# Pooling attention followed by mixture-of-depths: value pooling placed ahead of a gather, exponentials written contiguously, the second layer in one job, another order for batch 0

## The chip, the cores and the metric

The kernel runs on one core of a Trainium2 chip. Its engines are TensorE (PE: matmul; PEld: weight load), VectorE (DVE), ScalarE (ACT), GpSimd (POOL) and SyncE (SP); each works through its own instructions in order. The metric is the device time of one execution in microseconds (us); the median of the runs is compared.

## The reference

All values are fp32. B = 8 batches, H = 8 heads, S = 576 positions, D = 64, F = 1024, capacity 128.

```python
k_p = k.reshape(B, H, Sp, 8, D).mean(axis=3)         # 576 keys -> 72
v_p = v.reshape(B, H, Sp, 8, D).mean(axis=3)
attn = softmax(q @ k_p.T / sqrt(D)) @ v_p            # (B, H, S, D)
x = attn.transpose(0, 2, 1, 3).reshape(B, S, 512)
scores = x @ w_gate                                  # (B, S)
out = x.copy()
for b in range(B):
    top = the 128 positions with the largest scores[b]
    ye = relu(x[b, top] @ w1) @ w2                   # 512 -> 1024 -> 512
    out[b, top] = x[b, top] + sigmoid(scores[b, top])[:, None] * ye
```

## The kernel before, in words

The order of all instructions is written by hand; nothing is rescheduled. Batches go in pairs, an even one e and an odd one o. Each pair takes five steps u: two steps of 256 positions for e, one that holds the last 64 positions of both batches, and two steps of 256 positions for o. In step u the main loop runs the attention of that step (`attend`, L352, on PE into an accumulator pA, of which there are two; `norm`, L360 to L377, on DVE), then the jobs of slot 0, then the scores of step u+1 (`scores`, L323: PE writes four PSUM banks, ACT takes exponentials of them, eight instructions at L338), the stores of x, the transposes of q for step u+2 (L308), and the jobs of slots 1 to 4. A job is put in a slot of a step by `at(u, slot, job, ...)`; jobs of a slot run in the order in which they were put.

Per batch the jobs are these. `pool_k` (L230, L231, POOL) and `k_trans` (L236 to L242, DVE) make pooled keys. `pool_v` (L248 to L252, POOL) adds eight values of each of four heads; half 0 and half 1 are the two groups of four heads. Its last instruction (L252) multiplies by w_gate, and `gate_v` (L256, DVE) sums that product into the column of the tile vp that `attend` reads with the pooled values. When a batch's scores for the gate are complete, `row_bcast` (L416, PE) and `count` (L428 to L433, DVE) rank its 576 positions, holding an accumulator pA; `one_hot` (L440, PE; L441, L443, DVE) and `gather` (L451, PE; L453, DVE, tile tok; L455, POOL, tile idx; L457, an indirect DMA issued by POOL) fetch the 128 chosen rows from the output in DRAM into xr. `gate` (L467, DVE) and `x_trans` (L479, PE; copied to xg by ACT at L481) follow; then the dense jobs: `hidden` twice (L489, PE; relu at L491, ACT) and `finish` twice, 256 columns each (L502, PE; y at L503, DVE), and the scatter of y (L505, an indirect DMA on POOL's queue). Loads of k, q and v are issued by SP (v: L122, L123), stores of x by ACT.

Of the kernel before, what the change touches and what calls it, by code (L numbers as in the profile page):

```python
# [10 lines left out]
AF = mybir.ActivationFunctionType  # L11
OP = mybir.AluOpType
# [36 lines left out]
def direct_path(ctx, tc, q, k, v, moe_w_gate, moe_w1, moe_w2, moe_capacity, out, flag):  # L49
# [27 lines left out]
    G = 16  # L77
# [163 lines left out]
        nc.vector.tensor_reduce(out=y[:, :, 0:128:2], in_=x[:, :, 0:64, :], axis=AX.X, op=OP.add)  # L241
        nc.vector.tensor_reduce(out=y[:, :, 1:128:16], in_=x[:, :, 64:SP, :], axis=AX.X, op=OP.add)  # L242

    def pool_v(b, g, eng):
        x = VR[b, g]
        VP[b] = vps[b % 2]
        h = slice(HG * g, HG * g + HG)
        eng.tensor_tensor(out=x[:, :, 0:4, :], in0=x[:, :, 0:4, :], in1=x[:, :, 4:8, :], op=OP.add)  # L248
        eng.tensor_tensor(out=x[:, :, 0:2, :], in0=x[:, :, 0:2, :], in1=x[:, :, 2:4, :], op=OP.add)  # L249
        eng.tensor_tensor(out=VP[b][:, h, 0:D], in0=x[:, :, 0, :], in1=x[:, :, 1, :], op=OP.add)  # L250

        nc.gpsimd.tensor_tensor(out=x[:, :, 2, :], in0=VP[b][:, h, 0:D], in1=wg[:, h, :], op=OP.mult)  # L252
# [58 lines left out]
    def scores(u):  # L311
        b = steps_all[u][0]
        if b is None:
            parts = [(x, slice(QT4 * n, QT4 * n + QT4)) for n, x in enumerate(lasts(u))]
        else:
            parts = [(b, slice(0, TM))]
        p = [bank([128, 2, len(parts), G * (parts[0][1].stop)], i) for i in range(4)]
        for n, (x, t) in enumerate(parts):
            for s in range(2):
                for j in range(2):  # L320
                    for i in range(4):
                        r = slice(32 * i, 32 * i + 32)
                        nc.tensor.matmul(p[i][:, s, n, :], KT[x][r, j, s, :], QT[u][r, j, t, G * s : G * s + G],  # L323
                                         start=(j == 0), stop=(j == 1))
        if b is None:
            ET[u] = [work.tile([128, 2, len(parts), TL], FT, name=f"el{i}{len(parts)}") for i in range(4)]
            for i in range(4):
                nc.scalar.activation(ET[u][i].rearrange("p s n (g t) -> p (s n) g t", t=QT4),
                                     p[i].rearrange("p s n (t g) -> p (s n) g t", t=QT4), AF.Exp, scale=exp_scale)
        else:  # L330
            ET[u] = [[work.tile([128, 2, C], FT, name=f"et{i}{c}") for i in range(4)] for c in range(2)]
            for c in range(2):
                for i in range(4):
                    x = p[i].rearrange("p s one (n t c g) -> p (s one n) c g t", n=2, c=2, g=G)[:, :, c]
                    y = ET[u][c][i].rearrange("p s (n g t) -> p (s n) g t", n=2, g=G)
                    if c == 0:
                        x, y = (z.rearrange("p a g t -> p a t g") for z in (x, y))
                    nc.scalar.activation(y, x, AF.Exp, scale=exp_scale)  # L338

    def attend(a):  # L340
        u, x = chunks[a]
# [92 lines left out]

    def one_hot(b):

        p = accumulator()[:, 0, 0 : 2 * NC].rearrange("p (k c) -> p k c", k=2)
        for c in range(NC):
            for i in range(c, NC):
                nc.tensor.matmul(p[:, 0, c : c + 1], GE[b][i][:, c, :], ones, start=(i == c), stop=(i == NC - 1))  # L440
        nc.vector.tensor_tensor(out=p[:, 1, :], in0=CN[b], in1=p[:, 0, :], op=OP.subtract)  # L441
        OH[b] = work.tile([C, NC, cap], BF, name="oh", bufs=1)
        nc.vector.tensor_tensor(  # L443
            out=OH[b], in0=slots, in1=p[:, 1, :].rearrange("p (c one) -> p c one", one=1).to_broadcast([C, NC, cap]),
            op=OP.is_equal)
# [30 lines left out]
    def x_trans(b):  # L476
        p = bank([128, DB, cap])
        for d in range(DB):
            nc.tensor.transpose(p[:, d, :], XR[b][:, 128 * d : 128 * d + 128], ident[:cap, :cap])  # L479
        XG[b] = work.tile([128, DB, cap], FT, name="xg", bufs=1)  # L480
        nc.scalar.copy(out=XG[b], in_=p)  # L481

    def hidden(b, part, p):

# [5 lines left out]
                                 start=(d == 0), stop=(d == DB - 1))  # L490
        nc.scalar.activation(HT[b, part], p[:, 0 : FB // 2, :], AF.Relu)  # L491

    def finish(b, part, p):

        idx, g = GV[b]
        if part == 0:
            gate_end(b)
        c = slice(DM // 2 * part, DM // 2 * part + DM // 2)
        p = p.rearrange("p a b -> p (a b)")[:cap, 0 : DM // 2]
        for f in range(FB):  # L500
            n, m = divmod(f, FB // 2)
            nc.tensor.matmul(p, HT[b, n][:, m, :], w2[:, f, c], start=(f == 0), stop=(f == FB - 1))  # L502
        nc.vector.scalar_tensor_tensor(Y[b][:, c], p, g, XR[b][:, c], op0=OP.mult, op1=OP.add)  # L503
        if part == 1:
# [5 lines left out]
    def dense(b, i, first=False):  # L510

        p = accumulator()[:, 0, 0 : FB // 2 * cap].rearrange("p (a b) -> p a b", b=cap) if first else bank([128, FB // 2, cap])
        (hidden, finish)[i // 2](b, i % 2, p)

# [7 lines left out]
    for b, (steps_of, dense_of) in {
        0: (((2, 1), (3, 0), (3, 3), (5, 0)), ((5, 3, False), (5, 3, False), (6, 1, True), (7, 1, True))),
        1: (((5, 1), (6, 0), (6, 3), (7, 3)), ((8, 1, True), (9, 1, True), (9, 2, False), (10, 1, True))),
    }.items():
        for f, x in zip((row_bcast, one_hot, gather, x_trans), steps_of):
            at(*x, f, b)
        at(*steps_of[0], count, b)  # L530
        at(*steps_of[3], gate, b)
        for i, (u, slot, first) in enumerate(dense_of):
            at(u, slot, dense, b, i, first)
    for e in range(2, B, 2):
        s = 6 + 5 * (e // 2 - 1)
        o, last = e + 1, e + 2 == B
        for f in (row_bcast, count):
            at(s + 2, 1, f, e)
            at(s + 4, 0 if last else 1, f, o)
        at(s + 3, 0, one_hot, e)  # L540
        at(s + 3, 3, gather, e)
        at(s + 4, 3, x_trans, e)
        at(s + 4, 3, gate, e)
        if last:
            for i, f in enumerate((one_hot, gather, None, x_trans)):
                at(s + 5, 1, dense, e, i, i == 0)
                if f:
                    at(s + 5, 1, f, o)
            at(s + 5, 1, gate, o)
# [474 lines left out]
```

## Time and profile before

| | us |
|---|---|
| median of the 3 runs (303.97 to 305.81) | 304.64 |
| the profiled execution | 307.21 |
| its span, first to last instruction | 305.4 |
| PE busy | 232.1 (76%) |
| DVE busy | 139.3 (46%) |
| POOL busy | 130.7 (43%) |
| ACT busy | 76.9 (25%) |

Busy time is an average over stretches with different limits. The mean granted clock of TensorE is 0.903 of its full speed; the profiled execution has 1.8 us outside its span.

### The profile page before, as it was taken

The page shows a single profiled execution, that of the slowest core. Times are in us where ns is not written, and L with a number is a line of the kernel's source. Part 1 is how long each engine was busy: PE and PEld are TensorE (multiplying, and loading weights), DVE is VectorE, ACT ScalarE, POOL GpSimd, SP SyncE. Part 2 cuts the span into 40 slices and gives each one's busy share as a digit, 9 for nine tenths or more (in the row PEclk, how much of TensorE's full clock was granted, in tenths as well). Part 3 has the DMA queues.
Part 4 walks back from the last instruction along what each step waited for, and adds up shares of the span by engine and source line. Part 5 has one row for each costly group of instructions (what it writes and reads, how often), then busy time and mean ns, then how long its engine had stood idle before and what let it go on. Part 6 is the DMA issues. An engine that isn't in the chain of part 4 may idle for free.

```text
span 305.4 us, 7024 instructions
## 1 busy us (share of the span) xinstructions
PE 232.1 (76%) x2922; PEld 205.4 (67%) x2922; DVE 139.3 (46%) x416; ACT 76.9 (25%) x185; POOL 130.7 (43%) x135
## 2 busy tenths in 40 slices
PE   0488565389992979949992799789982799799990
PEld 0367455269871869839981589679972689698970
DVE  5977727450561381674331452853620631711111
ACT  9045431131310404413111224224210323100100
POOL 8589703970078910870257920753537000201101
PEclk9999977559997799977997599999997899999997
DMA  7998999935483652317733422122121002311001
GB/s 288 356 359 297 323 403 406 367 148 157 153 330 114 204 222 69 88 60 243 289 101 113 164 105 71 50 91 71 36 69 36 34 2 71 104 38 34 36 0 45
DMA packets 13528, 46.94 MB, mean 154 GB/s; under 512 B 1584, under 2 KB 1584, under 8 KB 11440
## 3 DMA queue, kind: packets, MB, share of 16 engines
q1 hardware_dynamic: 9008, 32.77, 30.0%
q10 hardware_dynamic: 3200, 9.44, 9.2%
q0 software_dynamic: 1280, 4.20, 4.2%
q8 instruction: 25, 0.41, 0.6%
q14 instruction: 15, 0.12, 0.1%
HBM read 34.87 MB, written 11.53 MB: 152 GB/s over the span
## 4 chain that ended last, share of the span: by engine, by line
PE 54%; POOL 13%; issue 11%; DVE 10%; DMA 8%; ACT 2%; ACTq 1%; POOLq 0%; DVEq 0%; SPq 0%
PE bank L502 13%; PE bank L323 11%; PE pA L489 9%; PE bank L489 8%; PE pA L352 8%; POOL vraw L248 4%; PE pA L502 4%; DMA qraw<-in_q_dram 3%; DMA xr<-out_dram,idx 2%; POOL vraw L249 2%; DMA out_dram<-xs 2%; ACT et L338 2%; DVE ge L432 1%; POOL vp L250 1%; DVE kh L236 1%
## 5 line engine op out<-in xcount | busy, mean ns | idle before, releaser
L338 ACT ACTIVATE et<-bank 128x256 f32<-128x256 f32 x128 | 49.0, 535 | 104.6 <-PE bank L323 104.6
L323 PE MATMUL bank<-qt,kt 32*128 32x256 f32 (+1 forms) x768 | 51.5, 412 | 13.9 <-DVE qt L308 12.1
L323 PEld LDWEIGHTS bank<-qt,kt 32*128 32x128 f32 x768 | 40.2, 222 | 18.7 <-POOL auxb L200 12.1
L352 PE MATMUL pA<-vp,et 128*64 128x66 f32 x1024 | 40.0, 240 | 12.9 <-DVE vp L256 7.1
L352 PEld LDWEIGHTS pA<-vp,et 128*64 128x64 f32 x1024 | 36.7, 152 | 16.5 <-DVE vp L256 6.0
L455 POOL TENSOR_SCALAR idx<-tok 128x1 int32<-128x1 f32 x8 | 1.8, 225 | 106.7 <-DVE tok L453 99.3
L502 PE MATMUL bank<-w,ht 128*128 128x256 f32 x176 | 39.7, 380 | 1.7 <-ACT et L338 1.7
L489 PE MATMUL bank<-xg,w 128*128 128x128 f32 x288 | 35.3, 284 | 4.5 <-ACT et L338 3.8
L489 PEld LDWEIGHTS bank<-xg,w 128*128 128x128 f32 x288 | 34.2, 199 | 5.7 <-ACT et L338 4.8
L502 PEld LDWEIGHTS bank<-w,ht 128*128 128x128 f32 x176 | 32.9, 190 | 6.1 <-ACT et L338 1.9
L248 POOL TENSOR_TENSOR vraw<-vraw 128x1024 f32<-128x1024 f32 x14 | 33.0, 2355 | 0.3
L489 PEld LDWEIGHTS pA<-xg,w 128*128 128x128 f32 x224 | 25.5, 192 | 3.0 <-issue 2.0
L489 PE MATMUL pA<-xg,w 128*128 128x128 f32 x224 | 26.9, 278 | 0.7 <-ACT xg L481 0.7
L503 DVE SCALAR_TENSOR_TENSOR y<-bank,g,xr 128x256 f32<-128x256 f32 x11 | 5.3, 484 | 48.3 <-PE bank L502 48.3
L505 POOL DMA_INDIRECT out_dram<-y,idx x8 | 9.1, 1142 | 41.6 <-DVE y L503 25.6
L432 DVE SCALAR_TENSOR_TENSOR ge<-pA,sc,before 128x128 bf16<-128x128 f32 (+3 forms) x40 | 18.4, 506 | 12.8 <-PE pA L416 12.8
L352 PE MATMUL pA<-vp,el 128*64 128x66 f32 x128 | 8.8, 260 | 19.5 <-DVE vp L256 18.7
L308 DVE STREAM_TRANSPOSE qt<-qraw 128x1024 f32<-128x1024 f32 (+1 forms) x24 | 23.0, 968 | 0.1
L368 DVE TENSOR_TENSOR xs<-pA,rzall 128x512 f32<-128x512 f32 x32 | 22.1, 691 | 1.1
L352 PEld LDWEIGHTS pA<-vp,el 128*64 128x64 f32 x128 | 7.1, 165 | 21.1 <-DVE vp L256 19.7
L360 DVE RECIPROCAL rzall<-pA 128x8 f32<-128x8 f32 (+1 forms) x37 | 7.6, 205 | 27.2 <-PE pA L352 27.2
L502 PE MATMUL pA<-w,ht 128*128 128x256 f32 x80 | 18.6, 386 | 0.0
(91 smaller groups left out, 249.2 us busy)
## 6 DMA issues: line engine op xcount, KB each, us to landing
kraw<-in_k_dram SPq DMA_DIRECT2D x8, 1152.0 KB, 15.9
qraw<-in_q_dram SPq DMA_DIRECT2D x8, 1152.0 KB, 7.5
vraw<-in_v_dram SPq DMA_DIRECT2D x16, 512.0 KB, 4.3
out_dram<-xs ACTq DMA_DIRECT2D x32, 256.0 KB, 4.1
w<-in_moe_w_dram SPq DMA_DIRECT2D x2, 2048.0 KB
vraw<-in_v_dram SPq DMA_DIRECT2D x16, 64.0 KB
out_dram<-xh ACTq DMA_DIRECT2D x8, 128.0 KB, 4.3
wg<-in_moe_w_gate_dram SPq DMA_DIRECT2D x1, 256.0 KB, 7.6
```

Source lines behind the costliest of these rows:

```text
L248: eng.tensor_tensor(out=x[:, :, 0:4, :], in0=x[:, :, 0:4, :], in1=x[:, :, 4:8, :], op=OP.add)
L249: eng.tensor_tensor(out=x[:, :, 0:2, :], in0=x[:, :, 0:2, :], in1=x[:, :, 2:4, :], op=OP.add)
L308: nc.vector.transpose(out=QT[u][:, :, n : n + x.shape[1], :].rearrange("p j t c -> p t j c"), in_=x)
L323: nc.tensor.matmul(p[i][:, s, n, :], KT[x][r, j, s, :], QT[u][r, j, t, G * s : G * s + G], start=(j == 0), stop=(j == 1))
L338: nc.scalar.activation(y, x, AF.Exp, scale=exp_scale)
L352: nc.tensor.matmul(PA[a][TL * t : TL * t + TL, g, E * n : E * n + E], e, VP[b][:, h, :], start=True, stop=True)
L360: nc.vector.reciprocal(rz, o[:, :, :, D])
L368: nc.vector.tensor_tensor(out=y[r, i, :].rearrange("p (g n d) -> p g n d", g=2, d=D), in0=o[:, :, :, 0:D], in1=rz.rearrange("p g (n one) - ...
L432: nc.vector.scalar_tensor_tensor(x, y, s, m, op0=OP.is_ge, op1=OP.mult, accum_out=k[:, c, 0:1])
L489: nc.tensor.matmul(p[:, n, :], w1[:, d, 128 * f : 128 * f + 128], XG[b][:, d, :], start=(d == 0), stop=(d == DB - 1))
L502: nc.tensor.matmul(p, HT[b, n][:, m, :], w2[:, f, c], start=(f == 0), stop=(f == FB - 1))
L505: i = nc.gpsimd.indirect_dma_start(out=out_rows, out_offset=bass.IndirectOffsetOnAxis(ap=idx[:, :1], axis=0), in_=Y[b], in_offset=None)
```

## The change

The diff has four parts. First, both halves of an odd batch's `pool_v` are put at (s+5, 0), ahead of the even batch's gather; before, half 0 stood behind that gather and half 1 behind the even batch's scatter. Batch 2's half 0 likewise moves ahead of gather(0), `gate_v` of batch 1 moves by one slot, and one multiplication of batch 0 goes from POOL to DVE. Second, the eight exponentials of a step all write their tile contiguously (before, the four with c = 0 read PSUM contiguously and wrote with a stride), and from step 6 on they go bank by bank. Third, `finish` is one job of 512 columns, save for batch 1, and several dense jobs stand at other slots. Fourth, batch 0's `count`, `one_hot` and `gather` have other places, and its `x_trans` stands behind the scores of step 6 and is copied by DVE.

```diff
-    def pool_v(b, g, eng):
+    def pool_v(b, g, eng, mult=nc.gpsimd):
...
-        nc.gpsimd.tensor_tensor(out=x[:, :, 2, :], in0=VP[b][:, h, 0:D], in1=wg[:, h, :], op=OP.mult)
+        mult.tensor_tensor(out=x[:, :, 2, :], in0=VP[b][:, h, 0:D], in1=wg[:, h, :], op=OP.mult)
...
-            for c in range(2):
-                for i in range(4):
-                    x = p[i].rearrange("p s one (n t c g) -> p (s one n) c g t", n=2, c=2, g=G)[:, :, c]
-                    y = ET[u][c][i].rearrange("p s (n g t) -> p (s n) g t", n=2, g=G)
-                    if c == 0:
-                        x, y = (z.rearrange("p a g t -> p a t g") for z in (x, y))
-                    nc.scalar.activation(y, x, AF.Exp, scale=exp_scale)
+            for c, i in [(c, i) for c in range(2) for i in range(4)] if u < 6 else [(c, i) for i in range(4) for c in range(2)]:
+                nc.scalar.activation(
+                    ET[u][c][i].rearrange("p s (n g t) -> p (s n) g t", n=2, g=G),
+                    p[i].rearrange("p s one (n t c g) -> p (s one n) c g t", n=2, c=2, g=G)[:, :, c], AF.Exp, scale=exp_scale)
...
-        p = accumulator()[:, 0, 0 : 2 * NC].rearrange("p (k c) -> p k c", k=2)
+        p = (accumulator()[:, 0, 0 : 2 * NC] if b else bank([C, 2 * NC])).rearrange("p (k c) -> p k c", k=2)
...
-        nc.scalar.copy(out=XG[b], in_=p)
+        if b == 0:
+            nc.vector.tensor_copy(out=XG[b], in_=p)
+        else:
+            nc.scalar.copy(out=XG[b], in_=p)
...
-    def finish(b, part, p):
+    def finish(b, part, parts, p):
...
-        c = slice(DM // 2 * part, DM // 2 * part + DM // 2)
-        p = p.rearrange("p a b -> p (a b)")[:cap, 0 : DM // 2]
+        c = slice(DM // parts * part, DM // parts * (part + 1))
+        p = p.rearrange("p a b -> p (a b)")[:cap, 0 : DM // parts]
...
-        0: (((2, 1), (3, 0), (3, 3), (5, 0)), ((5, 3, False), (5, 3, False), (6, 1, True), (7, 1, True))),
-        1: (((5, 1), (6, 0), (6, 3), (7, 3)), ((8, 1, True), (9, 1, True), (9, 2, False), (10, 1, True))),
...
+    at(3, 0, row_bcast, 0)
+    at(3, 0, count, 0)
+    at(3, 1, one_hot, 0)
+    at(3, 1, gather, 0)
+    at(5, 1, x_trans, 0)
+    at(5, 2, gate, 0)
+    at(5, 2, row_bcast, 1)
+    at(5, 2, dense, hidden, 0, 0)
+    at(5, 2, count, 1)
+    at(5, 3, dense, hidden, 0, 1)
+    at(6, 0, one_hot, 1)
+    at(6, 1, dense, finish, 0, 0, True)
+    at(6, 3, gather, 1)
+    at(7, 1, x_trans, 1)
+    at(7, 2, gate, 1)
+    at(7, 2, dense, hidden, 1, 0)
+    at(8, 2, dense, hidden, 1, 1)
+    at(9, 1, dense, finish, 1, 0, True, 2)
+    at(10, 2, dense, finish, 1, 1, False, 2)
...
-            for i in range(4):
-                at(s + 5 + i // 2, 1 + i % 2, dense, e, i, i % 2 == 0)
-            at(s + 7, 2, dense, o, 0)
-            at(s + 8, 1, dense, o, 1, True)
-            at(s + 8, 2, dense, o, 2)
-            at(s + 9, 2, dense, o, 3)
+            at(s + 5, 1, dense, hidden, e, 0, True)
+            at(s + 5, 2, dense, hidden, e, 1)
+            at(s + 6, 1, dense, finish, e, 0, True)
+            at(s + 7, 2, dense, hidden, o, 0)
+            at(s + 8, 1, dense, hidden, o, 1, True)
+            at(s + 9, 2, dense, finish, o, 0)
...
-            at(s + 5, 4, pool_v, y, 0, pool)
+            at(s + 5, 0, pool_v, y, 0, pool)
+            at(s + 5, 0, pool_v, y, 1, pool)
             at(s + 5, 4, k_trans, y)
-            at(s + 6, 4, pool_v, y, 1, pool)
...
-    at(3, 4, pool_v, 2, 0, pool)
+    at(3, 0, pool_v, 2, 0, pool)
+    at(3, 4, pool_v, 2, 1, pool)
-    at(4, 1, pool_v, 2, 1, pool)
...
-    at(6, 4, pool_v, 3, 0, pool)
+    at(6, 0, pool_v, 3, 0, pool)
+    at(6, 0, pool_v, 3, 1, pool)
     at(6, 4, k_trans, 3)
-    at(7, 1, pool_v, 3, 1, pool)
```

Three places show how the instructions stand. The first is POOL in the second pair, around the gather of batch 4 (`idx`, then the DMA into `xr`), its scatter (the DMA from `y`) and the value pooling of batch 5 (`vraw_72` and `vraw_73` are its two halves). Before:

```order
L455 TENSOR_SCALAR idx<-tok 128x1
L457 DMA xr<-out_dram,idx 128x512
L248 TENSOR_TENSOR vraw_72<-vraw_72 128x4x256
L249 TENSOR_TENSOR vraw_72<-vraw_72 128x4x128
L250 TENSOR_TENSOR vp_96<-vraw_72 128x4x64
L252 TENSOR_TENSOR vraw_72<-vp_96,wg 128x4x64
L505 DMA out_dram<-y,idx 4608x512
L248 TENSOR_TENSOR vraw_73<-vraw_73 128x4x256
L249 TENSOR_TENSOR vraw_73<-vraw_73 128x4x128
L250 TENSOR_TENSOR vp_96<-vraw_73 128x4x64
L252 TENSOR_TENSOR vraw_73<-vp_96,wg 128x4x64
L230 TENSOR_TENSOR kraw<-kraw 128x9x128
```

and after:

```order
L248 TENSOR_TENSOR vraw_72<-vraw_72 128x4x256
L249 TENSOR_TENSOR vraw_72<-vraw_72 128x4x128
L250 TENSOR_TENSOR vp_96<-vraw_72 128x4x64
L252 TENSOR_TENSOR vraw_72<-vp_96,wg 128x4x64
L248 TENSOR_TENSOR vraw_73<-vraw_73 128x4x256
L249 TENSOR_TENSOR vraw_73<-vraw_73 128x4x128
L250 TENSOR_TENSOR vp_96<-vraw_73 128x4x64
L252 TENSOR_TENSOR vraw_73<-vp_96,wg 128x4x64
L453 TENSOR_SCALAR idx<-tok 128x1
L455 DMA xr<-out_dram,idx 128x512
L506 DMA out_dram<-y,idx 4608x512
L230 TENSOR_TENSOR kraw<-kraw 128x9x128
```

Both halves now stand ahead of batch 4's gather and scatter, which follow each other. The second place is PE at steps 5 and 6, around the transposes of batch 0's gathered rows (`ident,xr`), the scores of step 6 (`qt,kt`) and batch 0's first hidden part (`xg,w`). Before:

```order
L352 MATMUL pA<-vp_96,el_679 64x66 x2
L479 MATMUL bank_710<-ident,xr 128x128 x4
L323 MATMUL bank_720<-qt_686,kt_97 128x256
L323 MATMUL bank_721<-qt_686,kt_97 128x256
L323 MATMUL bank_722<-qt_686,kt_97 128x256
L323 MATMUL bank_723<-qt_686,kt_97 128x256
```

and after:

```order
L323 MATMUL bank_712<-qt_690,kt_97 128x256
L323 MATMUL bank_713<-qt_690,kt_97 128x256
L477 MATMUL bank_749<-ident,xr 128x128 x4
L414 MATMUL pA<-ident,sc_116 128x128 x5
L490 MATMUL bank_765<-xg,w_125 128x128 x16
L490 MATMUL bank_797<-xg,w_125 128x128 x16
```

The transposes no longer stand between the attention of step 5 and the scores of step 6, but behind those scores, right ahead of batch 1's row_bcast (`sc_116`) and of both hidden parts. The third place is PE at step 10, where batch 1's second finish part (`w_126,ht`), batch 3's row_bcast (`sc_116`) and the attention of step 11 (`vp_95,et`) meet. Before:

```order
L323 MATMUL bank_1398<-qt_1299,kt_97 128x256
L323 MATMUL bank_1399<-qt_1299,kt_97 128x256
L502 MATMUL pA<-w_126,ht_1147 128x256 x4
L502 MATMUL pA<-w_126,ht_1302 128x256 x4
L416 MATMUL pA<-ident,sc_116 128x128 x5
L479 MATMUL bank_1466<-ident,xr 128x128 x4
L352 MATMUL pA<-vp_95,et_1416 64x66 x4
L352 MATMUL pA<-vp_95,et_1417 64x66 x4
```

and after:

```order
L323 MATMUL bank_1388<-qt_1308,kt_97 128x256
L323 MATMUL bank_1389<-qt_1308,kt_97 128x256
L414 MATMUL pA<-ident,sc_116 128x128 x5
L503 MATMUL bank_1445<-w_126,ht_1072 128x256 x4
L503 MATMUL bank_1445<-w_126,ht_1181 128x256 x4
L477 MATMUL bank_1456<-ident,xr 128x128 x4
L350 MATMUL pA<-vp_95,et_1406 64x66 x4
L350 MATMUL pA<-vp_95,et_1407 64x66 x4
```

Batch 3's row_bcast, on which its count on DVE waits, now stands ahead of the finish instead of behind it, and that finish writes a bank instead of an accumulator.

## Rows read from the trace of the kernel before

**Rows 1.** The page's first line.

```profile
span 305.4 us, 7024 instructions
```

**Rows 2.** The waits: engine and tile, releaser: us in total, times, longest.

```profile
PE pA L352 <- DVE vp L256: 25.8, 8, 5.9
...
DVE vp L256 <- POOL vraw L252: 20.0, 5, 6.1
```

**Rows 3.** Timeline of PE, second pair: start us, us, work [idle before <-releaser].

```profile
168.82 1.14 PE L352 MATMUL pA<-vp,el 128*64 128x66 f32 x14 [5.60 <-DVE vp L256]
169.89 3.80 PE L323 MATMUL bank<-qt,kt 32*128 32x256 f32 x32
...
175.98 3.84 PE L489 MATMUL bank<-xg,w 128*128 128x128 f32 x32 [1.11 <-ACT et L338]
...
182.48 2.01 PE L323 MATMUL bank<-qt,kt 32*128 32x256 f32 x32
...
198.74 3.72 PE L502 MATMUL bank<-w,ht 128*128 128x256 f32 x16 [1.67 <-ACT et L338]
```

**Rows 4.** Windows, one stretch: stretch, us, busy by engine, PEclk, DMA share, GB/s.

```profile
168.80:173.60 4.80, 4.78 (x46) 3.59 (x46) 2.40 (x7) 0.00 (x0) 4.72 (x3) 0.50 0.46 140
```

**Rows 5.** Timeline of POOL, second pair, same columns.

```profile
149.90 0.22 POOL L455 TENSOR_SCALAR idx<-tok 128x1 int32<-128x1 f32 x1 [13.39 <-DVE tok L453]
...
161.81 1.22 POOL L505 DMA_INDIRECT out_dram<-y,idx  x1 [4.67 <-DVE y L503]
163.07 2.34 POOL L248 TENSOR_TENSOR vraw<-vraw 128x1024 f32<-128x1024 f32 x1
...
168.27 2.62 POOL L230 TENSOR_TENSOR kraw<-kraw 128x1152 f32<-128x1152 f32 x1
```

**Rows 6.** Line L338 in two windows: ns of one least/median/most, first and last start.

```profile
L338 ACT ACTIVATE et<-bank x4: 633/669/682, 15.9 to 17.3; 128x256 f32<-128x256 f32 x4
...
L338 ACT ACTIVATE et<-bank x5: 377/409/682, 17.3 to 18.6; 128x256 f32<-128x256 f32 x5
```

**Rows 7.** Timeline of PE, first part.

```profile
57.83 1.09 PE L479 MATMUL bank<-ident,xr 128*128 128x128 f32 x4 [7.17 <-DMA xr<-out_dram,idx]
59.59 3.79 PE L323 MATMUL bank<-qt,kt 32*128 32x256 f32 x32 [0.68 <-ACT xg L481]
...
65.74 8.88 PE L489 MATMUL bank<-xg,w 128*128 128x128 f32 x64 [1.09 <-ACT et L338]
```

**Rows 8.** Timeline of POOL, first part.

```profile
44.82 0.24 POOL L455 TENSOR_SCALAR idx<-tok 128x1 int32<-128x1 f32 x1 [8.42 <-DVE tok L453]
50.85 1.23 POOL L457 DMA_INDIRECT xr<-out_dram,idx  x1 [5.79 <-issue]
```

**Rows 9.** The chain that ended last: start us, us, link.

```profile
34.74 9.53 DMA qraw<-in_q_dram
```

**Rows 10.** Line L457, issue to landing of its eight gathers.

```profile
DMA to landing us min/median/max: 3.3/3.5/7.2
```

**Rows 11.** Timeline of PE, first pair.

```profile
91.83 0.63 PE L479 MATMUL bank<-ident,xr 128*128 128x128 f32 x4 [0.87 <-DMA xr<-out_dram,idx]
...
99.38 1.14 PE L352 MATMUL pA<-vp,el 128*64 128x66 f32 x14 [5.88 <-DVE vp L256]
...
111.10 1.16 PE L352 MATMUL pA<-vp,et 128*64 128x66 f32 x32 [1.81 <-DVE ge L432]
...
135.64 3.79 PE L352 MATMUL pA<-vp,et 128*64 128x66 f32 x64 [4.47 <-DVE vp L256]
```

**Rows 12.** Timeline of DVE.

```profile
130.78 0.35 DVE L432 SCALAR_TENSOR_TENSOR ge<-pA,sc,before 128x128 bf16<-128x128 f32 x1
...
133.81 1.43 DVE L467 SCALAR_TENSOR_TENSOR y<-xr,wg 128x512 f32<-128x512 f32 x1
...
161.05 0.48 DVE L503 SCALAR_TENSOR_TENSOR y<-bank,g,xr 128x256 f32<-128x256 f32 x1 [2.97 <-PE bank L502]
```

**Rows 13.** Timeline of SP's DMA queue.

```profile
99.35 0.63 SPq L122 DMA_DIRECT2D vraw<-in_v_dram  x1
```

More of the change, by code (lines that the diff above doesn't have):

```diff
@@ L503, in finish @@
         nc.vector.scalar_tensor_tensor(Y[b][:, c], p, g, XR[b][:, c], op0=OP.mult, op1=OP.add)
-        if part == 1:
+        if part == parts - 1:
             i = nc.gpsimd.indirect_dma_start(
@@ L508, in finish, with dense @@
             scat[b] = [i]
-    def dense(b, i, first=False):
-        p = accumulator()[:, 0, 0 : FB // 2 * cap].rearrange("p (a b) -> p a b", b=cap) if first else bank([128, FB // 2, cap])
-        (hidden, finish)[i // 2](b, i % 2, p)
+    def dense(f, b, part, first=False, parts=1):
+        p = accumulator()[:, 0, :].rearrange("p (a b) -> p a b", b=128) if first else bank([128, 4, 128])
+        if f is hidden:
+            hidden(b, part, p[:, :, 0:cap])
+        else:
+            finish(b, part, parts, p)
     jobs = {}
@@ L523, in direct_path @@
     pool = nc.gpsimd
-    for b, (steps_of, dense_of) in {
-        0: (((2, 1), (3, 0), (3, 3), (5, 0)), ((5, 3, False), (5, 3, False), (6, 1, True), (7, 1, True))),
-        1: (((5, 1), (6, 0), (6, 3), (7, 3)), ((8, 1, True), (9, 1, True), (9, 2, False), (10, 1, True))),
[L527 to L533, printed above, removed]
+    at(3, 0, row_bcast, 0)
[17 more added lines that the diff above has]
+    at(10, 2, dense, finish, 1, 1, False, 2)
     for e in range(2, B, 2):
@@ L544, in direct_path @@
         if last:
[L545 to L549, printed above, removed]
-            for i in range(4):
-                at(s + 5, 1, dense, o, i)
+            for f, *x in ((dense, hidden, e, 0, True), (one_hot, o), (dense, hidden, e, 1), (gather, o),
+                          (dense, finish, e, 0), (x_trans, o), (gate, o), (dense, hidden, o, 0), (dense, hidden, o, 1),
+                          (dense, finish, o, 0)):
+                at(s + 5, 1, f, *x)
         else:
@@ L556, in direct_path @@
             at(s + 6, 3, gate, o)
-            for i in range(4):
-                at(s + 5 + i // 2, 1 + i % 2, dense, e, i, i % 2 == 0)
-            at(s + 7, 2, dense, o, 0)
-            at(s + 8, 1, dense, o, 1, True)
-            at(s + 8, 2, dense, o, 2)
-            at(s + 9, 2, dense, o, 3)
+            at(s + 5, 1, dense, hidden, e, 0, True)
[4 more added lines that the diff above has]
+            at(s + 9, 2, dense, finish, o, 0)
             x, y = e + 2, e + 3
@@ L596, in direct_path @@
     at(0, 2, load_k, 3)
-    at(2, 0, gate_v, 1, 0)
-    at(2, 0, gate_v, 1, 1)
+    at(2, 1, gate_v, 1, 0)
+    at(2, 1, gate_v, 1, 1)
     at(2, 1, load_v, 3, 0)
@@ L629, in direct_path @@
     pool_v(0, 0, nc.vector)
-    pool_v(0, 1, nc.vector)
+    pool_v(0, 1, nc.vector, nc.vector)
     load_k(2)
```

## Prediction

> **What bounds the kernel now.** The page's first line gives a span of 305.4 us [rows 1]; TensorE (PE) is busy for 232 of them, and the chain that ended last runs mostly through PE. So I ask where PE waits. The list of waits says that its largest wait is for the gate column of the value tile: eight waits, 25.8 us, up to 5.9 each; and that VectorE in turn waits 20.0 us for the POOL product (L252) ahead of that column [rows 2].
>
> The timeline of PE shows the place. In the second pair the attention of step 13 (the last 64 positions of both batches) stops for 5.60 us until 168.82; the scores behind it then take 3.80 us, where the same 32 matmuls take 2.01 us at 182.48 [rows 3]. The granted clock between 168.8 and 173.6 was 0.50, which is the 1.2 GHz level [rows 4]: an idle PE is paid for twice, by the wait and by slower matmuls behind it. The pattern stands three times, with 5.88 us in the first pair [rows 11] and 5.61 in the third.
>
> The timeline of POOL says why. Batch 4's `idx` starts at 149.90 after 13.39 us of idleness, so POOL was free from 136.5. Half 0 of batch 5's pooling follows the gather. Then POOL waits 4.67 us for the y of batch 4's finish, scatters at 161.81, and only at 163.07 begins half 1, which ends when the next work starts at 168.27: 5.2 us [rows 5]. The reader should see work standing behind a wait that it has nothing to do with, while the same queue was idle ahead of it.
>
> Before 75 us the limit is another: PE waits 7.17 us for batch 0's gathered rows until 57.83, and only then runs the scores of step 6, which don't need them [rows 7].
>
> **The change, part by part.** All sums go against the profiled execution's span.
>
> *Pooling ahead of the gather.* Two halves take 2 x 5.2 = 10.4 us. Begun at 136.5, they end at 146.9, 3.0 us ahead of where `idx` stood [rows 5]. Each pair loses its wait (5.88, 5.60, 5.61), and the clock behind it stays up: the scores go from 3.80 to 2.01 [rows 3], -1.8, and the attention of 1.14 us halves, -0.5. In the first pair I take -1.2 for the clock (between nothing and the 2.3 of the second). Cover: POOL is busy for only 43% of the span. If the work around it shrinks by 5 us, `idx` comes up to 2 us later than its rows are ready; the rows landed about 3.5 us after the issue [rows 10], that is near 155, while the finish ahead of the transposes ended at 161.05 [rows 12]. So a delay of 4 to 5 us stays hidden.
>
> *Exponentials.* Four with the strided write start over 1.4 us, 0.46 apart, and take 633 to 682 ns; in the next window, where four of five write contiguously, the median is 409 and the spacing 0.32 [rows 6]. Eight go from about 3.1 to 2.3 us. Bank by bank, the first bank is free after two instructions instead of five: the hidden job that waited 1.11 us and the finish that waited 1.67 [rows 3] no longer wait. With the faster row_bcast between, that is -1.4 in the second and third pair, and -1.6 once for the finish. Speaking against it, the Trainium skill ("Advanced Engine Details and Errata", PSUM Cachelines) says that a non-contiguous PSUM access significantly slows matmuls; the new form reads PSUM with a stride. By that rule, carried over to ACT, the exponentials gain nothing and some 4.5 us of bank waits stay. The rows show the form with the strided read as the faster one, so I go by them.
>
> *Second layer in one job.* The columns are the same: 2 x 3.72 us [rows 3] become one of about 7.4. I cost the matmuls at no change (bounds: -0.5 to +0.3 for each of seven). y is written in one instruction of twice 256 columns: 0.48 [rows 12] becomes about 0.75, +0.3 each time it is on the path; +0.5 in a pair.
>
> *First part (batch 0).* Now: rows 57.83, transposes 1.09, copy, scores 3.79, row_bcast, hidden from 65.74 for 8.88 us [rows 7], to 74.6. After: the scores stand ahead. If the rows still land at 57.8, hidden ends at 57.8 + 1.1 + 1.3 + 8.9 = 69.1: -5.5, the lower bound. But `idx` also comes earlier: its count stands ahead of its former place, and POOL, free at 36.4 (44.82 less 8.42 [rows 8]), has only the moved half of 5.2 us ahead: 41.6. The gather before started 5.79 us after it was ready, with no releaser shown [rows 8]. With that delay and the longest landing (7.2 [rows 10]) the rows are there at 54.8, without it and at 3.5 near 46.5. The scores of step 6 can't start before q of batch 2 has landed, at 34.74 + 9.53 = 44.27 [rows 9], and been transposed (2 to 3 us): near 47, ending at 51. Then transposes 1.1, copy or row_bcast 1.3, hidden 8.9: 62.3 at best. I take 64.1, in the middle of 62.3 and 66.1: -10.5 (bounds -5.5 and -12.3). The multiplication moved to DVE and the moved `gate_v` cost some 0.7 us there while PE waits for other things; if that cover is gone, 0.7.
>
> *First pair.* The accumulator that batch 1's count held kept the attention waiting 1.81 us at 111.10 [rows 11]; the row_bcast now stands elsewhere, ahead of a hidden job: -1.8. At 135.64 the attention waited 4.47 us, then took 3.79 us [rows 11]. The releaser named is the gate column, which on DVE stands behind batch 3's count, 130.78 to 133.81, and the gate [rows 12]. That count began only when the finish (3.72) and the row_bcast behind it were done; now the row_bcast is ahead of that finish, so it starts 3.7 us sooner: I take -3.2 of the wait (bounds 0 and -4.5) and -1.7 for the clock. **A new wait**: batch 1's transposes waited 0.87 us for their rows [rows 11], with a half finish of 3.72 us between gather and transposes as cover. The whole finish now stands ahead of the gather, and batch 0's scatter with it on POOL. Uncovered, the wait is 0.87 + 3.72 = 4.6, at a quick landing about 2: net +2.5 (bounds +1 and +4.7). Behind it PE's whole queue waits. Hidden then comes right behind the copy: +0.7 (0.68 at 59.59 [rows 7]).
>
> *Sum.* First part -10.5. First pair -5.9 - 1.2 - 1.8 - 3.2 - 1.7 + 2.5 + 0.7 + 0.3 = -10.3. Second pair -5.6 - 0.5 - 1.8 - 1.4 - 1.6 + 0.5 = -10.4. Third pair -5.6 - 0.5 - 1.8 - 1.4 + 0.5 = -8.8. Together -40.0: the span becomes 265.4. The execution had 1.8 us outside its span: 267.2. It lay 2.6 above the median of the runs shown, so the median should be 264.6.
>
> **The rivals.**
> - *Batch 0's rows land no earlier*, since the DMA or the unexplained delay before the gather decides, not `idx`. For: 5.79 us of idleness without a releaser [rows 8] and a longest landing of 7.2 against 3.5. The first part gives 5.5 instead of 10.5: 269.6.
> - *Gathers late behind the pooling.* The work around shrinks, POOL's 10.4 us don't, and `idx` is delayed by more than the 4 to 5 us of cover. 3 us of new wait in three pairs: 273.6. Against: 3.0 us of margin and the cover behind it.
> - *Slower than before.* An odd batch's v lands late, and the pooling, now ahead of the gather, stops it, the transposes and PE's queue. Place: POOL ahead of `idx`; price: 1 us of PE for each us beyond margin and cover (about 8). It decides when three pairs lose 40 us: 13 + 8 = 21 us late each. Against: batch 5's last load is issued at 99.35 [rows 13], and POOL takes it up at 136.5.
> - *The exponentials' part does not do what it says*: the strided read eats the gain; bank waits of 1.1, 1.67 and the like stay: 269.
> - *Wider matmuls stream faster.* A hidden job of 32 records at 128 columns takes 3.84, that is 0.94 ns a column; a finish half of 16 at 256 takes 3.72, 0.91 [rows 3]. 3% more would give -0.2 for each of seven; a tenth, -0.7 each: 259.7. The Trainium skill ("TensorE: Matmul & The Clock Gate", Back-to-back issue gap) gives 81 ns at 128 columns and 131 ns at 512, a column at 0.40 of the price; by it seven finishes save 4 us each and the sum would be 236, an estimate. The 3% between 128 and 256 speaks against that.
>
> **How the numbers follow.** Chances: my forecast 0.63 (its own range 259 to 269); rows of batch 0 late 0.12; gathers late 0.12; exponentials 0.06; wider matmuls 0.05; slower 0.02. The range from 255 to 277 takes in the two larger delays and their sum with the bounds of the new wait, and leaves out 0.2. A measurement of this kernel tells about 0.5% from no change. Faster 0.96, the same 0.01, and 0.03 for slower, the 0.02 and a little for a delay that I don't see.
>
> **What would show it.** Right: the wait of PE for the gate column gone from 25.8 to under 5; scores behind step 13 near 2.0; `idx` of batch 0 near 42, hidden of batch 0 done by 64; all exponentials near 0.4; a wait of 2 to 5 us ahead of batch 1's transposes. Wrong: POOL busy up to a late `idx` in each pair, with PE waiting for gathered rows; batch 0's rows still landing after 55; a wait for banks that stays; finishes that take other than 7.4.

## The result, and the profile after

The changed kernel takes 267.43 us (median of 4 runs, 267.29 to 269.28), the kernel before 305.23 (4 runs). The ratio is 0.8775, with an interval from 0.8718 to 0.8831: faster. The forecast was 264.6 us in a range from 255 to 277. Medians are of all runs of a kernel; in experiments 3 and 8 one run was over 1.5% slower than the fastest, and without it their medians are 279.08 and 273.22.

The page of the profiled execution (267.35 us) begins with the span, then busy time by engine:

```profile
span 265.6 us, 6793 instructions
...
PE 220.5 (83%) x2810; PEld 177.0 (67%) x2810; DVE 139.3 (52%) x411; ACT 64.4 (24%) x184; POOL 130.4 (49%) x134
```

The span is 265.6 us where 265.4 was forecast. The median came out 2.8 us above the forecast because I took 2.6 us off the profiled execution, as it lay before; this one lay at its median.

The list of waits, with the columns of [rows 2]:

```profile
PE pA L350 <- DVE vp L256: 9.6, 6, 4.3
...
PE bank L477 <- DMA xr<-out_dram,idx: 2.8, 1, 2.8
```

PE's wait for the gate column is down from 25.8 us to 9.6, of which one wait of 4.33 stands at the very start, where 1.51 stood before. Beside the 4.33 there are four of 1.08 to 1.34 us, which experiment 10 takes up. The timeline of PE in the second pair answers [rows 3]:

```profile
144.17 1.15 PE L350 MATMUL pA<-vp,el 128*64 128x66 f32 x30 [1.09 <-DVE vp L256]
145.25 2.01 PE L323 MATMUL bank<-qt,kt 32*128 32x256 f32 x32
...
147.99 3.84 PE L490 MATMUL bank<-xg,w 128*128 128x128 f32 x32
...
165.43 7.13 PE L503 MATMUL bank<-w,ht 128*128 128x512 f32 x16
```

The attention of step 13 waits 1.09 us instead of 5.60, the scores behind it take 2.01 us instead of 3.80, and neither the hidden job nor the finish behind the row_bcast waits for a bank. The finish of 512 columns takes 7.13 us, against 2 x 3.72. The timeline of POOL shows the other half, and answers [rows 5]:

```profile
123.79 2.36 POOL L248 TENSOR_TENSOR vraw<-vraw 128x1024 f32<-128x1024 f32 x1
...
133.63 0.68 POOL L252 TENSOR_TENSOR vraw<-vp,wg 128x256 f32<-128x256 f32 x1
134.40 0.22 POOL L453 TENSOR_SCALAR idx<-tok 128x1 int32<-128x1 f32 x1
134.89 1.08 POOL L455 DMA_INDIRECT xr<-out_dram,idx  x1 [0.27 <-POOL idx L453]
143.46 1.20 POOL L506 DMA_INDIRECT out_dram<-y,idx  x1 [7.49 <-DVE y L504]
```

Half 0 begins at 123.79, half 1 ends at 134.3, and `idx` follows without idleness. POOL then idles ahead of the scatter, with nothing behind it that PE waits for. The margin of 3 us ahead of `idx` that I had worked out is gone, as forecast for a shorter kernel, and nothing on PE waits for the rows of this gather.

The first part answers [rows 7] and [rows 8], first on PE:

```profile
20.21 3.79 PE L350 MATMUL pA<-vp,et 128*64 128x66 f32 x64 [4.33 <-DVE vp L256]
...
52.41 3.05 PE L323 MATMUL bank<-qt,kt 32*128 32x256 f32 x32 [2.94 <-DVE kt L242]
56.17 1.12 PE L477 MATMUL bank<-ident,xr 128*128 128x128 f32 x4 [0.71 <-ACT et L334]
...
58.14 8.28 PE L490 MATMUL bank<-xg,w 128*128 128x128 f32 x64
```

on DVE:

```profile
17.01 2.72 DVE L252 TENSOR_TENSOR vraw<-vp,wg 128x256 f32<-128x256 f32 x1
...
49.08 1.25 DVE L308 STREAM_TRANSPOSE qt<-qraw 128x1024 f32<-128x1024 f32 x1 [1.09 <-DMA qraw<-in_q_dram]
...
52.05 0.21 DVE L242 TENSOR_REDUCE kt<-kh 128x32 f32<-128x64 f32 x1
```

and on POOL:

```profile
16.64 2.80 POOL L230 TENSOR_TENSOR kraw<-kraw 128x1152 f32<-128x1152 f32 x1 [0.67 <-DMA kraw<-in_k_dram]
...
43.85 0.24 POOL L453 TENSOR_SCALAR idx<-tok 128x1 int32<-128x1 f32 x1 [3.07 <-DVE tok L451]
44.83 1.23 POOL L455 DMA_INDIRECT xr<-out_dram,idx  x1 [0.74 <-POOL idx L453]
```

Batch 0's hidden jobs end at 66.42 instead of 74.62. But the first attention starts only at 20.21, behind a multiplication that took 2.72 us on DVE; the scores of step 6 start at 52.41, because q of batch 2 landed at 49.1 (not 44.3) and its keys are transposed behind that on DVE. In the first pair PE shows, in answer to [rows 11]:

```profile
85.01 1.09 PE L477 MATMUL bank<-ident,xr 128*128 128x128 f32 x4 [2.78 <-DMA xr<-out_dram,idx]
86.77 5.73 PE L490 MATMUL bank<-xg,w 128*128 128x128 f32 x32 [0.67 <-ACT xg L482]
...
119.17 2.09 PE L350 MATMUL pA<-vp,et 128*64 128x66 f32 x64 [1.08 <-DVE vp L256]
```

The new wait is there, 2.78 us; the 4.47 us at step 11 are 1.08. The windows of two stretches (columns as in [rows 4]) show the clock:

```profile
86.77:90.00 3.23, 3.23 (x15) 3.23 (x16) 0.49 (x2) 0.07 (x1) 3.15 (x2) 0.50 0.30 101
144.00:147.10 3.10, 2.93 (x62) 2.55 (x62) 2.09 (x9) 0.02 (x1) 3.08 (x2) 1.00 0.60 183
```

Behind the new wait the hidden job ran at a granted clock of 0.50 (1.2 GHz), behind the pooling's old place it is now 1.00 (2.4 GHz). The exponentials, all of the step's eight in one form, as in [rows 6]:

```profile
L334 ACT ACTIVATE et<-bank x128: 377/408/454, 15.9 to 213.6; 128x256 f32<-128x256 f32 x128
```

### The profile page after: what moved, and what is told of

The parts are those of the page before. It is cut to its first block, busy times and chain, and to the rows that moved or that the text cites. A ratio compares the mean times of both kernels' runs of the same rounds, so it can differ in the third digit from the quotient of the medians.

```text
span 265.6 us, 6793 instructions
## 1 busy us (share of the span) xinstructions
PE 220.5 (83%) x2810; PEld 177.0 (67%) x2810; DVE 139.3 (52%) x411; ACT 64.4 (24%) x184; POOL 130.4 (49%) x134
## 4 chain that ended last, share of the span: by engine, by line
PE 57%; POOL 14%; DVE 12%; issue 10%; DMA 4%; ACT 1%; POOLq 0%; DVEq 0%; ACTq 0%
PE bank L490 12%; PE bank L503 12%; PE bank L323 9%; PE pA L350 7%; PE pA L490 7%; PE pA L503 7%; POOL vraw L248 4%; DVE xs L366 2%; DMA qraw<-in_q_dram 2%; POOL kraw L230 2%; POOL vraw L249 2%; DMA xr<-out_dram,idx 2%; DVE kh L236 1%; POOL vraw L252 1%; PE pA L438 1%
## 5 line engine op out<-in xcount | busy, mean ns | idle before, releaser
L334 ACT ACTIVATE et<-bank 128x256 f32<-128x256 f32 x128 | 37.1, 411 | 75.0 <-PE bank L323 75.0
L490 PE MATMUL bank<-xg,w 128*128 128x128 f32 x352 | 44.2, 288 | 1.6 <-ACT xg L482 1.4
L490 PEld LDWEIGHTS bank<-xg,w 128*128 128x128 f32 x352 | 42.8, 203 | 3.1 <-ACT xg L482 2.0
L503 PE MATMUL bank<-w,ht 128*128 128x512 f32 (+1 forms) x80 | 32.0, 553 | 0.2
L503 PE MATMUL pA<-w,ht 128*128 128x512 f32 (+1 forms) x64 | 25.1, 545 | 0.0
L503 PEld LDWEIGHTS bank<-w,ht 128*128 128x128 f32 x80 | 14.8, 191 | 14.4 <-issue 13.4
L230 POOL TENSOR_TENSOR kraw<-kraw 128x1152 f32<-128x1152 f32 x7 | 18.6, 2661 | 9.6 <-DMA kraw<-in_k_dram 9.5
L490 PE MATMUL pA<-xg,w 128*128 128x128 f32 x160 | 19.2, 278 | 0.7 <-ACT xg L482 0.7
L503 PEld LDWEIGHTS pA<-w,ht 128*128 128x128 f32 x64 | 11.8, 190 | 11.2 <-issue 10.7
L249 POOL TENSOR_TENSOR vraw<-vraw 128x512 f32<-128x512 f32 x14 | 17.8, 1272 | 1.1
```

The lines of the kernel that those rows point to most:

```text
L334: nc.scalar.activation(ET[u][c][i].rearrange("p s (n g t) -> p (s n) g t", n=2, g=G), p[i].rearrange("p s one (n t c g) -> p (s one n) c g ...
L490: nc.tensor.matmul(p[:, n, :], w1[:, d, 128 * f : 128 * f + 128], XG[b][:, d, :], start=(d == 0), stop=(d == DB - 1))
```

## The experiments

Spans are of one profiled execution each; the changed kernel's is 265.6. "More" and "less" are differences of such spans, with the difference of the medians beside them where it tells something else. The eight runs of the changed kernel (in the result and in run 12) had spans from 264.4 to 267.7, so a difference of 3 us between two single spans can be chance.

**1. The pooling put back.**

```diff
-            at(s + 5, 0, pool_v, y, 0, pool)
-            at(s + 5, 0, pool_v, y, 1, pool)
+            at(s + 5, 4, pool_v, y, 0, pool)
             at(s + 5, 4, k_trans, y)
+            at(s + 6, 4, pool_v, y, 1, pool)
```

(and batch 3's halves at (6, 4) and (7, 1)).

> The changed kernel with only the odd batches' value pooling put back: half 0 behind the gather, half 1 behind the scatter. My theory: the three waits of about 5.6 us for the gate column come back, with 1.8 us of slower scores and 0.5 of slower attention behind each: 20 to 28 us more than the changed kernel's 267.4, about 291. The rival, that the other parts (exponentials, first part, finish) carry the gain and the pooling's wait would be hidden under them: under 8 us more, 275 or less.

Measured: 285.36 us, ratio to before 0.9274 (0.9207 to 0.9341), span 285.0: 19.4 more (17.9 by the medians). PE's timeline, steps 8 and 13:

```profile
94.62 1.16 PE L350 MATMUL pA<-vp,el 128*64 128x66 f32 x32
...
152.97 1.14 PE L350 MATMUL pA<-vp,el 128*64 128x66 f32 x14 [5.61 <-DVE vp L256]
```

In the second and third pair the wait is back with 5.61 us each. In the first it is not: the attention at 94.62 follows a hidden job of 5.39 us that the new order puts there, and the pooling ends beside it. The rival falls; my 20 to 28 was a little too much, for that reason.

**2. The pooling alone**, the same edit made on the kernel before.

> The kernel before with only the odd batches' value pooling moved ahead of the gather. My theory: about 24 us less than before, some 281, with the gate-column wait of PE down from 25.8 us to about 9 in total. The rival of late gathers: POOL's 10.4 us in front of the gather come back as a wait of the transposes for the gathered rows in each pair, so 10 us or less are gained (295 or more) and PE's wait for those rows grows from 8 us to over 15.

Measured: 283.84 us, ratio 0.9249 (0.9186 to 0.9312), span 280.8: 24.6 less than 305.4. Three rows of its list of waits:

```profile
PE pA L352 <- DVE vp L256: 9.8, 7, 4.5
...
PE bank L479 <- DMA xr<-out_dram,idx: 6.9, 1, 6.9
...
PE bank L489 <- ACT et L338: 4.9, 3, 1.7
```

The gate-column wait went from 25.8 to 9.8 as expected; PE's wait for gathered rows is 6.9, not over 15, so the gathers are not late. The wait of hidden jobs for banks has grown from 3.8 to 4.9 us, at the same three places as before.

**3. The exponentials as before**, in form and order, the rest of the change kept.

```diff
...
+            for c in range(2):
+                for i in range(4):
...
+                    if c == 0:
+                        x, y = (z.rearrange("p a g t -> p a t g") for z in (x, y))
...
```

> The changed kernel with the exponentials of before: four with the strided write first, all in the order c then bank. My theory: the bank waits of 1.1 to 1.7 us ahead of the hidden jobs and a finish come back, 4 to 6 us more than 267.4, about 272. The rival that they are hidden (ACT is busy for a quarter of the span): under 1 us more. The rival that the strided PSUM read costs: faster than 267.4.

Measured: 279.38 us, ratio 0.9133 (0.905 to 0.9216), span 275.6: 10.0 more (12.0 by the medians), twice what I expected. There are five waits for banks of 1.58 to 1.68 us, 8.2 together. Two of them, at steps 8 and 10:

```profile
99.54 3.84 PE L493 MATMUL bank<-xg,w 128*128 128x128 f32 x32 [1.65 <-ACT et L339]
...
118.72 3.72 PE L506 MATMUL bank<-w,ht 128*128 128x256 f32 x16 [1.67 <-ACT et L339]
```

The kernel before showed three such waits, at steps 13, 15 and 18 (and one of 1.09 in the first part). At steps 8 and 10 it waited for no bank, since its jobs there wrote the accumulator pA:

```profile
103.61 3.84 PE L489 MATMUL pA<-xg,w 128*128 128x128 f32 x32
...
126.47 3.72 PE L502 MATMUL pA<-w,ht 128*128 128x256 f32 x16
```

So the two further waits come with the change's own order, which has a hidden job at step 8 and a finish at step 10 write a bank right behind the row_bcast. The rest of the 10.0 lies mainly in the first part, where batch 0's transposes wait 2.23 us for ACT instead of 0.71.

**4. Batch 0's transposes ahead of the scores again.**

```diff
-    at(5, 1, x_trans, 0)
+    at(5, 0, x_trans, 0)
```

> The changed kernel with batch 0's transposes back ahead of the scores of step 6 (one job from slot 1 to slot 0 of step 5). The gathered rows now land near 52 (issue at 44.8, 7.7 us), the scores ran from 52.4 behind k and q of batch 2. My theory: the transposes and the copy in front delay the scores, and the hidden job then stands behind the scores, so 1 to 3 us more than 267.4. The rival that this order alone made the 8 us of the first part: 5 us or more. The rival that only the earlier gather did: within 0.5 us.

Measured: 268.01 us, ratio 0.8721 (0.8649 to 0.8793), span 266.7. PE:

```profile
21.30 3.79 PE L350 MATMUL pA<-vp,et 128*64 128x66 f32 x64 [5.35 <-DVE vp L256]
...
53.23 1.08 PE L477 MATMUL bank<-ident,xr 128*128 128x128 f32 x4 [0.89 <-DMA xr<-out_dram,idx]
55.09 3.80 PE L323 MATMUL bank<-qt,kt 32*128 32x256 f32 x32 [0.78 <-DVE xg L480]
...
59.94 7.58 PE L490 MATMUL bank<-xg,w 128*128 128x128 f32 x64
```

From the first attention to the end of hidden are 46.2 us (21.30 to 67.52); in the changed kernel also 46.2 (20.21 to 66.42). So the place of the transposes brings nothing here, and the rival holds: the rows now land near 53, and the scores could not start before 52.4 anyway. What is left is the rows' earlier landing. `idx` starts only 1.0 us sooner than before (43.85 for 44.82 [rows 8]); the larger part is the pause between `idx` and the gather, 5.79 us before and 0.74 now. Run 2 keeps the old order and has the pause too, and there the profile names a releaser:

```profile
51.70 1.23 POOL L457 DMA_INDIRECT xr<-out_dram,idx  x1 [5.48 <-DMA out_dram<-xs]
```

In the kernel before and in run 2 the gather waits over 5 us there, by run 2's row for stores of x to land; in every run with the new order it waits less than 1 us. Which stores these are, and why the gather's new place escapes them, is not shown.

**5. The one multiplication back on POOL.**

```diff
-    pool_v(0, 1, nc.vector, nc.vector)
+    pool_v(0, 1, nc.vector)
```

> The changed kernel with the one multiplication of batch 0's half 1 back on POOL. In the changed kernel it took 2.72 us on DVE, 17.01 to 19.73, beside POOL's first pooling step of k (16.64 to 19.44), and the first attention started at 20.21 instead of 17.44. My theory: DVE is slowed by POOL's work at the same time, so on POOL the product takes 0.68 and the first attention starts near 17.5: 2 to 2.8 us less, about 265. The rival that the delayed pooling of k and v of batch 1 on POOL takes it back before step 6: within 0.5 us of 267.4. The rival that the start does not matter since the loads of batch 2 decide at 52: the same, with a longer wait ahead of the scores of step 6.

Measured: 264.51 us, ratio 0.8658 (0.8606 to 0.8709), span 261.8: 3.8 less (2.9 by the medians). PE and then POOL:

```profile
17.46 0.69 PE L350 MATMUL pA<-vp,et 128*64 128x66 f32 x16 [1.74 <-DVE vp L256]
```

```profile
17.11 0.68 POOL L252 TENSOR_TENSOR vraw<-vp,wg 128x256 f32<-128x256 f32 x1 [1.14 <-DVE vp L250]
```

The product takes 0.68 us on POOL, the first attention starts at 17.46, and the gain lasts to the end.

**6. The finish in two parts again**, back to back in the same slot.

```diff
     def dense(f, b, part, first=False, parts=1):
+        if f is finish and parts == 1:
+            dense(f, b, 0, first, 2)
+            dense(f, b, 1, False, 2)
+            return
```

> The changed kernel with each finish in two parts of 256 columns, back to back in the slot of the one job. My theory: 7.13 us become 3.72 + 3.62 = 7.34, the last y is shorter by 0.3: between -1 and +1.5 us, so no change that can be told. The rival that wide matmuls made much of the gain (a column at 512 far cheaper than at 128): 10 us or more slower.

Measured: 268.17 us, ratio 0.878 (0.8727 to 0.8833), span 265.6: no change. The rival of cheap wide matmuls falls.

**7. Batch 1's gather ahead of batch 0's finish.**

```diff
+    at(6, 1, gather, 1)
     at(6, 1, dense, finish, 0, 0, True)
-    at(6, 3, gather, 1)
```

> The changed kernel with batch 1's gather ahead of batch 0's finish on PE, and so ahead of its scatter on POOL. My theory: the rows of batch 1 then land 7 us earlier, the wait of 2.78 us at 85.0 goes, and with it the lower clock of the hidden job behind it (5.73 us instead of 3.84): 4 to 5 us less, about 263, less some 0.5 for a wait for the one-hot tile. The rival that the transposes then wait for something else, or that the gather cannot start earlier because POOL pools batch 3's values until 74.8: 0 to 2 us less.

Measured: 265.28 us, ratio 0.8703 (0.8628 to 0.8778), span 262.4: 3.2 less. By the medians it is 2.2, and the runs, 263.93 to 267.61, overlap with the changed kernel's 267.29 to 269.28; I had expected 4 to 5, the rival 0 to 2. PE:

```profile
83.64 0.66 PE L477 MATMUL bank<-ident,xr 128*128 128x128 f32 x4 [0.46 <-ACT el L328]
85.68 3.84 PE L490 MATMUL bank<-xg,w 128*128 128x128 f32 x32 [1.38 <-ACT xg L482]
```

In this execution the wait for the rows is gone and the hidden job takes 3.84 us instead of 5.73. A wait of 1.38 us for ACT's copy is left, which I had not counted.

**8. The order of the exponentials alone put back**, c then bank, all contiguous.

```diff
-            for c, i in [(c, i) for c in range(2) for i in range(4)] if u < 6 else [(c, i) for i in range(4) for c in range(2)]:
+            for c, i in [(c, i) for c in range(2) for i in range(4)]:
```

> The changed kernel with contiguous exponentials, but in the order of before (c, then bank) in all steps. My theory: eight take 2.3 us instead of 3.1, and the first bank is free after five of them, 1.6 to 1.7 us in, instead of after two, 0.7: the row_bcast covers most of it, so waits of 0.2 to 0.5 us in some five places, 1 to 2 us more than 267.4. The rival that the order, not the form, removed the bank waits: 4 us or more.

Measured: 274.21 us, ratio 0.8964 (0.8881 to 0.9047), span 271.4: 5.8 more. The same two places:

```profile
98.87 3.84 PE L490 MATMUL bank<-xg,w 128*128 128x128 f32 x32 [0.93 <-ACT et L334]
...
117.31 3.72 PE L503 MATMUL bank<-w,ht 128*128 128x256 f32 x16 [0.93 <-ACT et L334]
```

My 1 to 2 us were too little; the rival holds. The five waits are 0.87 to 0.93 us each, 4.5 together. Of the exponentials' 10.0 us, the order is worth 5.8 and the form 4.2 by these spans; by the five waits alone it is 4.5 and 3.7. Which of the two is larger is not clear of the spread of the runs.

**9. Three places mended**: the edits of 5 and 7, and

```diff
-    at(4, 1, k_trans, 2)
+    at(3, 3, k_trans, 2)
```

> The changed kernel with three places mended: the multiplication of batch 0 back on POOL, batch 1's gather ahead of batch 0's finish, and batch 2's key transposes on DVE right behind batch 0's gather instead of behind the q transposes of step 6. My theory: the first two add up, spans 3.8 and 3.2 us shorter, and the scores of step 6, which waited 2.9 us for the keys, start 1 to 2 us sooner: 258 to 261. The rival that they are alternatives, because the loads of q and k of batch 2 decide when the first part ends: 263 or more.

Measured: 259.66 us, ratio 0.8527 (0.8497 to 0.8557), span 255.4. PE:

```profile
48.09 2.01 PE L323 MATMUL bank<-qt,kt 32*128 32x256 f32 x32
...
134.40 1.15 PE L350 MATMUL pA<-vp,el 128*64 128x66 f32 x30 [1.09 <-DVE vp L256]
```

The scores of step 6 start at 48.09 without a wait. By the medians it is 7.5 us below the changed kernel beside it (267.18), where runs 5 and 7 alone gave 2.9 and 2.2: as far as the spread of the runs tells, the savings add.

**10. The gate column earlier**, on top of 9.

```diff
-            at(s + 4, 4, gate_v, x, 0)
+            at(s + 4, 2, gate_v, x, 0)
...
-            at(s + 6, 4, gate_v, y, 0)
+            at(s + 6, 0, gate_v, y, 0)
```

(the same for half 1).

> The kernel of the last run with the gate column's sums of each later batch put ahead of y and of the gate product on DVE, two slots earlier for even and one step part earlier for odd batches. My theory: four waits of 1.08 to 1.35 us of PE for that column, which are left in the changed kernel because DVE first works through y and the gate product, go: 4 to 4.5 us less than the last run. The rival that DVE then waits for POOL's product and holds y back, or that the wait moves to the next release: 1 us or less.

Measured: 255.79 us, ratio 0.8385 (0.8349 to 0.8422), 3.9 less than 9; span 253.8, 1.6 less. PE, and the row of the waits:

```profile
76.89 1.08 PE L477 MATMUL bank<-ident,xr 128*128 128x128 f32 x4 [1.89 <-DMA xr<-out_dram,idx]
78.65 6.15 PE L490 MATMUL bank<-xg,w 128*128 128x128 f32 x32 [0.68 <-ACT xg L482]
...
134.43 1.16 PE L350 MATMUL pA<-vp,el 128*64 128x66 f32 x32
```

```profile
PE pA L350 <- DVE vp L256: 2.8, 5, 0.7
```

The wait at step 13 is gone. In this execution the rows of batch 1 landed late in spite of the earlier gather and cost 1.89 us and a slow hidden job (6.15 us), so run 7's gain is not had in every execution. The spans show less than the medians because run 9's profiled execution (257.19) was the fastest of its five. This is the fastest version: 4.3% below the changed kernel beside it (267.18).

**11. The new order alone**: 1, 3, 5 and 6 together.

> The changed kernel with the pooling, the exponentials, the two-part finish and the multiplication put back, so that only the other order of batch 0 and 1 and of the last pair is left of the change. If the parts simply add (spans: pooling 19.4 us, exponentials 10.0, multiplication -3.8, finish 0): a span of 291. By the sum of my prediction, 10.5 + 2.7 in the first part (with the slow multiplication out) and 3.2 net in the first pair: 289 to 293. The rival that the parts cover each other, so that the new order alone brings little while the pooling's wait stands: 298 or more.

Measured: 290.66 us, ratio 0.953 (0.9499 to 0.9561), span 289.5. Steps 8 and 10 on PE:

```profile
93.65 0.68 PE L353 MATMUL pA<-vp,el 128*64 128x66 f32 x14 [0.15 <-DVE vp L256]
...
98.63 3.84 PE L493 MATMUL bank<-xg,w 128*128 128x128 f32 x32 [1.68 <-ACT et L339]
...
117.82 3.72 PE L506 MATMUL bank<-w,ht 128*128 128x256 f32 x16 [1.68 <-ACT et L339]
```

291 by adding the parts, 289.5 measured: taken out of the changed kernel, they are nearly independent. The order alone removes the pooling's wait in the first pair (0.15 left of 5.88). And it brings the two bank waits of steps 8 and 10 with it, with the old pooling still in place.

**12. The changed kernel again.**

> The changed kernel itself, unchanged, beside the other three on the same chip. Both theories: 267.4 within 1.5 us; it is the mark that the others are read against.

Measured: 267.18 us, ratio 0.8784 (0.873 to 0.8839).

## Why the prediction was right

**The whole.** -40.0 us of span forecast, -39.8 measured. Cut at two places that rows give, the end of batch 0's hidden jobs and of step 13's attention: the first part lost 8.2 us (74.62 to 66.42; forecast 10.5), the next 16.4 (95.34 to 78.90; forecast 10.3 + 5.6 + 0.5 = 16.4), the rest 15.2 (135.44 to 120.28; forecast 13.1). The mechanism of the pooling is shown; that the sum is exact to 0.2 us is luck, since errors of both signs cancel, and since the profiled execution of the kernel before was a long one: between the medians the change is 37.8 us. Three of the signs that I had named were missed: the gate column's wait is 9.6, not under 5; `idx` of batch 0 starts at 43.85, not near 42 (41.62 once run 5 has put the multiplication back); and its hidden jobs end at 66.42, not by 64.

**Pooling ahead of the gather: right.** I credited it with 22.9 us; alone it brings 24.6 (run 2), taken out it costs 19.4 (run 1). The difference agrees with the first pair, where the new order covers the wait anyway (runs 1 and 11). That the slow clock is the second half of the price shows in the scores: 2.01 us behind the step of the last positions, in each pair.

**Exponentials: right as a term, incomplete as a mechanism.** I counted -4.4, from the three waits that the profile of before showed, and those waits are gone. Taken out of the changed kernel, the new exponentials are worth 10.0 (run 3), for there five jobs wait. The step that I missed, a term that I put at nothing, is that the change's own order has two more jobs write a bank right behind the row_bcast, at steps 8 and 10: with the old exponentials that order costs two waits of about 1.7 us (runs 3 and 11). The stall of the pooling did not hide them: run 2 takes the stall out under the old order, has no bank wait at steps 8 and 10, and only the one at step 13 grows, from 1.11 to 1.62. The order by banks and the form are worth about half each (run 8). The Trainium skill's rule on PSUM ("Advanced Engine Details and Errata", PSUM Cachelines), carried over to ACT, had the strided read as the slower; the trace has it at a median of 408 ns (377 to 454) over all 128 instructions, against 633 to 682 for the strided write, so the rule, which speaks of matmuls, does not decide here.

**Second layer in one job: right.** 7.13 for 7.34 us, 0.75 us for y, and no change when undone (run 6). The wide matmuls did not become cheap by the column: 7.13 us for 16 records of 512 are 0.87 ns a column, against 0.91.

**First part: right in sign, in part wrong in its cause.** Of the 10.5 I put 5.5 on the scores that no longer stand behind the rows. Run 4 puts them back behind the transposes and loses nothing. Against the kernel before, its rows are there 4.6 us sooner (53.23 for 57.83), the wait of 1.09 us for ACT is gone, and the hidden jobs take 7.58 instead of 8.88: that is the 7.1 us by which its hidden jobs end sooner. The earlier rows come with the new order: run 11, the order alone, has batch 0's hidden jobs done at 67.0; what in that order lets the gather go sooner stays open (run 4). And "cost some 0.7 us there while PE waits for other things" failed: the moved multiplication cost 2.72 us on the path of the first attention, and 3.8 in the end (run 5). That q of batch 2 would be there at 44.3 held for the kernel before only.

**First pair.** The wait of the count (1.81) is gone, the 4.47 became 1.08 (forecast 1.3), the new wait is 2.78 (forecast 3.4). What I missed is the clock behind that new wait: the hidden job takes 5.73 us instead of 3.84, the same double price that I had charged to the old wait. Run 7's execution has both back; in run 10's the wait stands again with 1.89.

**Rivals.** Late rows of batch 0 and late gathers did not come: the longest wait for rows is that 2.78. The chance of the strided read eating the gain (0.06) was well below what the Trainium skill's rule would suggest, and the rows were right.

## What to carry to other kernels

Look at each in-order queue for work whose inputs are ready but which stands behind something that waits, and price the wait with the slower matmuls behind it. A part of a change can be worth more in the changed kernel than in the kernel before: here the new order had two more jobs wait for banks, which the new exponentials free in time. So count the places where a part will act in the new order, and price each from the producer's own durations. Moving one small instruction to an idle engine still needs a look at what the other engines do in just that stretch.

## What was not expected of the hardware

The product of 128 x 256 took 2.72 us on DVE (17.01 to 19.73) beside POOL's pooling step of k (16.64 to 19.44), and 0.68 us on POOL in run 5: DVE ended 0.3 us after POOL did. The instruction ahead of it on DVE, a sum of the same size (L250), took 0.42 us at 16.55. The Trainium skill ("SBUF — State Buffer", Who interferes with whom) says that a DVE instruction with two SBUF inputs contends with a GpSimd instruction that reads SBUF, and that the order of issue decides which of the two blocks. The rows agree with that: the product began 0.4 us after POOL's step and ended behind it; that the shared port is the cause was not tested apart from the placement.
